# One group for the head sums and v pairs, a fifth product buffer, and one gate tile moved ahead of the second token group

## The chip, the cores and the metric

The kernel runs on one core of a Trainium2 chip. The metric is device time in microseconds (us) of one launch, as a median over runs of the same program. TensorE (PE) multiplies, VectorE (DVE) does elementwise work, ScalarE (ACT) does activations and moves results out of PSUM, GpSimd (POOL) does small statistics and issues some DMAs, and the queue of SyncE (SP) issues most other DMAs. Each engine runs its own instructions in program order.

## The reference

A layernorm of x (2048 tokens, 512 features) feeds two branches, and both are added to x. All arrays are bfloat16.

```python
xn = _layernorm(x)
return x + _A_ref(xn, A_wqkv, A_wo) + _B_ref(xn, B_w_in, B_w_sp, B_b_sp, B_w_out)

# A: 32 heads of 16 features, each token attends to 8 tokens: its own and those 2, 4, ... 14 before it
logits = einsum('bhsd,bhswd->bhsw', q, kg) * Dh ** -0.5   # masked where the index is below 0
o = einsum('bhsw,bhswd->bhsd', softmax(logits), vg)       # then o @ wo

# B: a gated unit that mixes over all tokens, Fh = 688
z = _gelu(x @ w_in)
z1, z2 = z[..., :Fh], _layernorm(z[..., Fh:])
g = einsum('ts,bsf->btf', w_sp, z2) + b_sp
return (z1 * g) @ w_out
```

## The kernel before

All data stays on the chip between load and store. The 2048 tokens are 16 tiles of 128; two halves (`th` 0 and 1) of 1024 tokens are used for attention, and four token groups (`b` 0 to 3) of 512 tokens for the q and k projections.

The order is written out by hand in two lists of short names, `ten` (lines 455 to 461, mostly PE and ACT work) and `vec` (lines 444 to 454, mostly DVE and POOL work). The function `advance` walks both lists; `needs` (line 464) says which names must have been recorded before another, and `do` (line 577) maps a name to its helper. So the order in `ten` is the order of PE and of ACT, and the order in `vec` is that of DVE and POOL. The hardware waits come from the buffers that the instructions read and write.

The names that matter here:

- `zN` is the matrix product of token tile N for z2 (line 209, 8 matmuls of 344 columns into one PSUM pair), `hN` its gelu on ACT (line 220), and `qN` the sum of its squares on ACT (line 225). `yN` is the product of tile N for z1 with its gelu (lines 244 to 246).
- `kBC` (line 254, 8 matmuls) projects token group B: C = 0, 1 are the two parts of q and C = 2, 3 the two of k. The helper copies the PSUM pair on ACT (line 256). `k1x` reads the transposed tiles 4 to 7.
- `vN` (line 269) projects a pair of v features in 32 matmuls, each of which uses 32 columns of the PE array at one of four positions (`tile_position`). ACT copies the result (line 271).
- `mTW`, `jTW`, `fTW`, `dTW`, `pTW`: the product of q with two shifted copies of k for half T and window pair W on DVE (line 289), and the adding up of the four feature chunks, by DVE (lines 292, 293) or with its first step as a DMA that POOL issues (`d`, line 298).
- `STW` (line 305) sums that product over the features of each head, with four matmuls that also use 32 columns each, and ACT moves the result (line 307) into `a_sb`. `xT` (line 315 on) is the softmax of half T, after its four head sums.
- `tN` is the DMA transpose of normalized tile N into `xnT` (line 205), `WN` a DMA transpose of two tiles of w_sp into one of three buffers `wsp` (line 368 on), `MN` the mixing product of output tile N (line 374), and `gN` the gate on DVE (line 382). `zsN` and `znN` are the statistics and the normalization of z2, by four tiles. `aT.N` are the twelve steps of attention of half T on DVE, and `Q`, `F` the output products and the additions of x.

PSUM is shared out by hand. Three pairs of banks `mm` are taken in turn by every z, k, v, y and M, and two banks `aux` in turn by the transposes at the start and by the head sums. So a z, k or v has to wait until ACT has emptied the pair taken three allocations earlier.

SBUF is full, so products share memory with other things. `prod` lists four homes, and `home` (line 277) says which one a product takes: two buffers of their own (0 and 1), the first 8192 columns of the z1 tile (2), and a part of the weights that is no longer read (3). The z1 tile has 16 x 768 = 12288 columns: it holds x in its first 8192 (`xs`) and normalized tiles in the other 4096 (`xn`) until they are transposed, and z1 later. A product that takes a home anew waits for the head sum of the product that had it.

```python
home = {(0, 0): 0, (0, 1): 1, (0, 2): 2, (0, 3): 0, (1, 0): 1, (1, 1): 0, (1, 2): 1, (1, 3): 3}
```

Of the kernel before, what the change touches and what calls it, by code (L numbers as in the profile page):

```python
# [7 lines left out]
BF16 = mybir.dt.bfloat16  # L8
# [5 lines left out]
P = 128  # L14
S = 2048
D = 512
NT = S // P
C = D // P
# [6 lines left out]
HS = S // 2  # L25
# [6 lines left out]
FP = (MF + 1) * P  # L32
# [6 lines left out]
def kernel(  # L39
# [22 lines left out]
    sb = ctx.enter_context(tc.tile_pool(name="sb", bufs=1))  # L62
# [35 lines left out]
    prod = [sb.tile([P, 2 * C * HS], BF16, name=f"prod{n}")[:] for n in range(2)]  # L98
    z2_r = sb.tile([P, NT * FH], BF16, name="z2")
    z2 = z2_r[:].rearrange("p (i f) -> p i f", i=NT)  # L100
    ot = [z2_r[:, n * D:(n + 1) * D] for n in range(12)]
    z1_r = sb.tile([P, NT * FP], BF16, name="z1")
    z1u = z1_r[:].rearrange("p (i f) -> p i f", i=NT)
    prod.append(z1_r[:, 0:2 * C * HS])
    prod.append(wts[:, C * FH:C * (FH + 4 * D)])
    xs = z1_r[:, 0:NT * D].rearrange("p (i d) -> p i d", i=NT)
    xn = [z1_r[:, NT * D + n * D:NT * D + (n + 1) * D] for n in range(8)]
    vp = sb.tile([P, DH, 2, HALO + GS], BF16, name="vp")
    a_sb = sb.tile([P, 2, W, GS], BF16, name="a_sb")
    wsp_r = [sb.tile([P, NT * 2 * P], BF16, name=f"wsp{n}") for n in range(3)]  # L110
    wsp = [r[:].rearrange("p (k t) -> p k t", k=NT) for r in wsp_r]

    mm = [ps.tile([P, 2, D], F32, name=f"mm{n}") for n in range(3)]
    aux = [ps.tile([P, D], F32, name=f"aux{n}") for n in range(2)]
# [159 lines left out]
        G.dma_start(vp[H:P, :, :, 0:HALO], vp[0:P - H, :, :, GS:GS + HALO])  # L274
        G.dma_start(vp[0:H, :, 1, 0:HALO], vp[P - H:P, :, 0, GS:GS + HALO])

    home = {(0, 0): 0, (0, 1): 1, (0, 2): 2, (0, 3): 0, (1, 0): 1, (1, 1): 0, (1, 2): 1, (1, 3): 3}

    def prod_ops(th, w2):
        pr = prod[home[th, w2]].rearrange("p (w c s) -> p w c s", w=2, c=C)  # L280
# [124 lines left out]
    def load_res(th):  # L405
        (SP if th else A).dma_start(xr[th], x2[th * HS:(th + 1) * HS, :].rearrange("(i p) d -> p i d", p=P))

    xr = [wsp_r[n][:].rearrange("p (i d) -> p i d", i=8) for n in (2, 0)]

    def gated_full(i, po, start, stop, cols=slice(0, D)):  # L410
        th, t0 = i // 8, (i % 8) * P
# [33 lines left out]
    for i in range(5, NT):  # L445
# [7 lines left out]
        a1.0 a1.1 g11 a1.2 a1.3 g12 a1.4 g13 a1.5 g14 a1.6 a1.7 g15 X1 a1.8 a1.9 F0 a1.10 a1.11 F1 F2  # L453
    """.split()
    ten = """
        T0 T1 B GL z0 z1 h0 T3 h1 z2 h2 z3 h3 LZ k00 k01 q0 k02 q1 k03 q2 z4 q3 h4 k10 k12 k11 k13
        W0 q4 k20 z5 h5 q5 k21 z6 h6 q6 k22 z7 h7 q7 k23 z8 h8 q8 k30 z9 h9 q9 k31 z10 h10 q10 S00 v0
        k32 z11 h11 q11 k33 z12 h12 q12 z13 h13 q13 v1 S01 S02 v2 z14 h14 z15 h15 q14 v3
        q15 v4 v5 v6 v7 S03 S10 y0 y1 M0 EL H e0 M1 EG y2 y3 y4 EL1 i0 EG1 M2 y5 y6 y7 y8 y9 y10 S11 S12 S13 M3 y11 M4 y12
        M5 W4 W5 y13 y14 y15 O4 EL2 e1 M6 O0 O1 M7 W6 i1 M8 O2 M9 W7 M10 O3 M11 M12 X0 M13 M14 M15 Q0 Q2 Q3  # L460
    """.split()
# [2 lines left out]
    def needs(n):  # L464
        k, a = n[0], n[1:]
        i = int(a) if a.isdigit() else 0
        if k == "T":
            return [f"n{i}"]
        if k == "z" and a.isdigit():
            return [[f"T{i}"], ["T1", "n2"], ["z1"], ["T3"]][i] if i < 4 else [f"t{i}"]  # L470
        if n == "GL":
            return ["T1"]
        if k == "q":
            return [f"h{i}"]
        if k == "h":
            return [f"z{i}"]
        if k == "k":
            last = 4 * int(a[0]) + 3
            return [f"T{last}" if last < 4 else f"t{last}"]
        if k == "v":  # L480
            return ["t15", "LW"]
        if k == "S":
            return ["p" + a]
        if k == "m":
            b = 2 * int(a[0])
            r = ([f"k{x}3" for x in (b, b + 1)] + ["K"]) if b else ["k03", "k12"] + (["k13"] if a != "00" else [])
            prev = [p for p in prods[:prods.index(n)] if home[int(p[1]), int(p[2])] == home[int(a[0]), int(a[1])]]
            return r + (["S" + prev[-1][1:]] if prev else []) + (["v7", "z15"] if a == "13" else [])
        if k == "j":
            return ["k13"]  # L490
        if k in "fdp":
            return ["m" + a]
        if k == "K":
            return ["k13"]
        if n[:2] == "zs":
            return [f"q{int(n[2:]) + x}" for x in range(4)]
        if k == "x":
            return [f"S{a}{w}" for w in range(4)]
        if k in "euic":
            return ["xeui"["euic".index(k)] + a]  # L500
        if k == "a":
            r = ["c" + a[0], "H", "S12"] + (["S13"] if a not in ("0.0", "0.1") else [])
            return r + ([f"y{x}" for x in range(NT)] if a[2:] == "11" else [])
        if k == "H":
            return [f"v{x}" for x in range(8)] + ["d12"]
        if k == "M":
            return [f"zn{x}" for x in range(NT)] + [f"W{i // 2}", "B"] + ([f"g{i - 3}"] if i >= 3 else [])
        if k == "g":
            return [f"M{i}", f"y{i}"]
        if k == "W":  # L510
            return [f"M{2 * i - 5}"] if i >= 3 else ["t15"]
        if k == "y":
            return [f"t{NT - 1}", "LW", "S02"]
        if k == "B":
            return ["T1"]
        if k == "O":
            return [f"y{x}" for x in range(NT)] + ["S13"]
        if k == "Q":
            return [["a0.11", "g7", "O4"], ["g7"], ["a1.11", "g15", "F0"], ["F2"]][i]
        if k == "F":  # L520
            return [f"Q{[0, 0, 2][i]}", f"X{i // 2}"]
        if k == "X":
            return ["M11" if i == 0 else "M13"]
        return []
# [171 lines left out]
    def advance(n):  # L696

        own = next(x for x in lists if n in x)
        while n not in done:
            first = next(x for x in own if x not in done)  # L700
            for x in needs(first):
                if x not in done:
                    assert x not in own, (first, x)
                    advance(x)
            do(first)
# [36 lines left out]
```

## Time and profile before

| | us |
|---|---|
| median of 3 runs | 202.16 (202.12 to 202.41) |
| the profiled execution, whole | 202.3 |
| its span, first to last instruction | 200.6 |
| PE busy | 195.9 |
| DVE busy | 175.7 |
| ACT busy | 96.0 |
| POOL busy | 38.7 |

The granted TensorE clock was 0.997 on average over the span. All times in the profile count from the start of the span; 1.7 us of the profiled execution lie around it. In the views, "PE mm L254 x8" is eight matmuls of line 254 that write a tile named mm, and a bracket at the end of a row of the timeline is the idle time of that engine ahead of it, with what ended the idle time. The chain of waits follows the work that ended last back to the beginning.

### The profile page before, as it was taken

How to read it: one execution, taken by the hardware profiler on the slowest of the kernel's cores; microseconds unless marked ns; L12 is line 12 of the kernel's file. 1: busy time of each engine (PE TensorE's matmuls, PEld its weight loads, DVE VectorE, ACT ScalarE, POOL GpSimd, SP SyncE). 2: the span in 40 equal slices, each digit the busy share in tenths (PEclk: the TensorE clock that was granted, in tenths of full speed). 3: DMA queues.
4: the chain of work that ended last, by engine and by line, in shares of the span. 5: the costliest groups of instructions: out<-in, count | busy, mean ns of one | idle time of the engine just before them, and what ended most of it. 6: DMA issues, size and time to landing. Idle time of an engine off the chain costs nothing.

```text
span 200.6 us, 3841 instructions
## 1 busy us (share of the span) xinstructions
PE 195.9 (98%) x1587; PEld 118.2 (59%) x1587; DVE 175.7 (88%) x192; ACT 96.0 (48%) x149; POOL 38.7 (19%) x62
## 2 busy tenths in 40 slices
PE   7999999999999999999999999999999999999993
PEld 2645555555656666666566666666666654444652
DVE  4887879999899799999979999999999799897333
ACT  3869879998998647885533264311222110000000
POOL 4366681138660431600000000000000000000000
PEclk9999999999999999999999999999999999999998
DMA  6999459399653837999979099996949611712023
GB/s 183 288 250 197 102 117 303 106 184 206 132 110 29 184 65 146 186 101 89 248 168 192 9 259 281 156 259 128 266 82 272 135 43 39 252 65 105 5 103 105
DMA packets 64289, 30.84 MB, mean 154 GB/s; under 512 B 53440, under 2 KB 62512, under 8 KB 64144
## 3 DMA queue, kind: packets, MB, share of 16 engines
q1 hardware_dynamic: 59296, 19.23, 46.4%
q0 software_dynamic: 1904, 6.59, 16.5%
q10 hardware_dynamic: 3072, 4.78, 8.8%
q8 instruction: 12, 0.20, 0.4%
q14 instruction: 5, 0.04, 0.1%
HBM read 10.03 MB, written 2.10 MB: 60 GB/s over the span
## 4 chain that ended last, share of the span: by engine, by line
PE 88%; DMA 6%; DVE 3%; POOL 1%; issue 0%
PE mm L374 37%; PE mm L209 16%; PE mm L254 10%; PE mm L269 7%; PE mm L413 7%; PE mm L425 5%; DMA z<-in_A_x_dram 4%; DMA xnT<-z 2%; PE aux L413 2%; DVE stats L182 1%; PE mm L562 1%; PE mm L419 1%; PE aux L305 1%; DVE z L196 1%; POOL rstd L187 1%; PE aux L562 0%
## 5 line engine op out<-in xcount | busy, mean ns | idle before, releaser
L374 PE MATMUL mm<-z,wsp 128*128 128x344 bf16 x512 | 75.7, 309 | 0.0
L374 PEld LDWEIGHTS <-wsp 128*128 128x128 bf16 x512 | 50.0, 98 | 24.9 <-issue 0.4
L209 PE MATMUL mm<-wts,xnT 128*128 128x344 bf16 x256 | 40.5, 309 | 0.0
L377 ACT ACTIVATE qk<-mm,b_col 128x688 bf16<-128x688 f32 x16 | 13.3, 834 | 49.8 <-PE mm L374 49.8
L347 DVE TENSOR_TENSOR prod<-vp,a_sb 128x4096 bf16<-128x4096 bf16 x16 | 36.0, 2284 | 0.0
L209 PEld LDWEIGHTS <-xnT 128*128 128x128 bf16 x256 | 24.6, 98 | 14.0 <-issue 0.8
L254 PE MATMUL mm<-xnT,wts 128*128 128x512 bf16 x128 | 29.1, 379 | 0.3 <-DMA xnT<-z 0.2
L289 DVE TENSOR_TENSOR prod<-qk 128x4096 bf16<-128x4096 bf16 (+1 forms) x14 | 27.1, 1979 | 0.1
L351 DVE TENSOR_TENSOR prod<-prod,prod 128x8192 bf16<-128x8192 bf16 x6 | 26.5, 4420 | 0.1
L254 PEld LDWEIGHTS <-wts 128*128 128x128 bf16 x128 | 14.3, 114 | 13.1 <-issue 0.9
L256 ACT CAST qk<-mm 128x1024 bf16<-128x1024 f32 x16 | 16.2, 1011 | 4.8 <-PE mm L254 3.0
L413 PE MATMUL mm<-wts,qk 128*128 128x512 bf16 (+1 forms) x65 | 14.7, 371 | 0.0
L269 PE MATMUL mm<-xnT,wts 128*32 128x512 bf16 x256 | 14.6, 381 | 0.0
L246 ACT ACTIVATE z<-mm 128x688 bf16<-128x688 f32 x16 | 11.8, 745 | 4.5 <-PE mm L209 4.5
L182 DVE BATCH_NORM_STATS2 stats<-z 128x6 f32<-128x512 bf16 x16 | 10.9, 683 | 3.4 <-DMA z<-in_A_x_dram 3.4
L413 PEld LDWEIGHTS <-qk 128*128 128x128 bf16 x85 | 8.1, 98 | 9.2 <-issue 0.6
L220 ACT ACTIVATE z<-mm 128x688 bf16<-128x688 f32 x16 | 11.9, 744 | 1.8 <-PE mm L209 1.8
L225 ACT ACTIVATE z_junk<-z 128x688 bf16<-128x688 bf16 x16 | 12.4, 778 | 0.3
L269 PEld LDWEIGHTS <-wts 128*32 128x32 bf16 x256 | 9.3, 139 | 4.6 <-issue 0.6
L430 DVE TENSOR_TENSOR z<-mm,wsp 128x512 bf16<-128x512 f32 (+1 forms) x8 | 5.0, 653 | 8.0 <-PE mm L425 4.8
L298 POOL DMA_DIRECT2D prod<-prod x8 | 7.1, 933 | 20.9 <-DVE prod L289 19.5
L425 PE MATMUL mm<-wts,xnT 32*128 32x512 bf16 x160 | 10.7, 375 | 0.0
(93 smaller groups left out, 186.2 us busy)
## 6 DMA issues: line engine op xcount, KB each, us to landing
prod<-prod POOLq DMA_DIRECT2D x8, 512.0 KB, 5.7
wts<-in_A_wo_dram ACTq DMA_DIRECT2D x4, 512.0 KB, 5.5
out_dram<-z SPq DMA_DIRECT2D x9, 128.0 KB, 1.7
z<-in_A_x_dram SPq DMA_DIRECT2D x4, 256.0 KB, 4.4
wts<-in_A_wqkv_dram SPq DMA_DIRECT2D x2, 512.0 KB, 7.0
z<-z POOLq DMA_DIRECT2D x2, 512.0 KB, 5.6
wsp<-in_A_x_dram ACTq DMA_DIRECT2D x1, 1024.0 KB, 6.3
wsp<-in_A_x_dram SPq DMA_DIRECT2D x1, 1024.0 KB, 5.3
```

The costliest lines, as they stand in the source:

```text
L182: V.bn_stats(stats[:, i, :], xs[:, i, :])
L209: PE.matmul(pz[:, hh, 0:FHALF], xnT[:, kc, i * P:(i + 1) * P], w_z2[:, hh, kc] if part else w_z1[:, kc, hh * FHALF:(hh + 1) * FHALF], star ...
L254: PE.matmul(pq[:, cc, :], w_c[:, kc], xnT[:, kc, t0:t0 + D], start=(kc == 0), stop=(kc == C - 1))
L256: A.copy(qk[b // 2][:, a, 2 * c2:2 * c2 + 2, o:o + D], pq[:])
L269: PE.matmul(pv[32 * g:32 * g + 32, dd, :], w, r, start=(kc == 0), stop=(kc == C - 1), tile_position=(0, 32 * g))
L289: ops.append(lambda ww=ww, k=k, c=c: V.tensor_tensor(pr[:, ww, c], q[:, c], k[:, c], ALU.mult))
L347: return lambda: V.tensor_tensor(dst, vp[:, :, th, off:off + GS], a_sb[:, th, w].unsqueeze(1).broadcast_to([P, DH, GS]), ALU.mult)
L351: return lambda: V.tensor_tensor(dst, dst, x, ALU.add)
L374: PE.matmul(pg[:, hh, 0:FHALF], w[:, k, (j % 2) * P:(j % 2 + 1) * P], z2[:, k, hh * FHALF:(hh + 1) * FHALF], start=(k == 0), stop=(k == NT ...
L377: A.activation(g.rearrange("p (a b) -> p a b", a=2), pg[:, :, 0:FHALF], ACT.Identity, bias=b_col[:, j:j + 1])
L413: PE.matmul(po[:, cols], uT[th][:, m, t0:t0 + P], wout[:, m, cols], start=(start and m == 0), stop=(stop and m == MF - 1))
L425: PE.matmul(pos[g], op[32 * g:32 * g + 32, th, d, s * P:(s + 1) * P], wo_r[32 * g:32 * g + 32, d, :], start=(start and d == 0), stop=(stop ...
```

## The change

Two things are reordered and the buffers are shared out anew.

In `ten`, z5 with its gelu moves ahead of the second token group's chunks (k10, k12, k11, k13), where z4 stood alone. Every later z keeps its distance to the k chunks and so comes one place earlier. The first half's head sums S00, S01, S02 and the v pairs v0 to v3, which stood in three places among the z and k of the last tiles, now all follow z15, just ahead of v4 to v7, S03 and S10. The squares q13, q14 and q15 are spread between the v pairs.

Product (0, 3) gets a new home 4. It takes the last 8192 columns of a z1 tile that is lengthened by 4096 columns: those of `xn` and those of the third w_sp buffer, which is now a part of this tile. The homes of (1, 0), (1, 1) and (1, 2) become 0, 1, 0 in place of 1, 0, 1. In `needs`, the load W2, which fills that third buffer first, now needs S03.

```diff
-    z1_r = sb.tile([P, NT * FP], BF16, name="z1")
-    z1u = z1_r[:].rearrange("p (i f) -> p i f", i=NT)
+    z1_all = sb.tile([P, NT * FP + NT * 2 * P], BF16, name="z1")
+    z1_r = z1_all[:, 0:NT * FP]
+    z1u = z1_r.rearrange("p (i f) -> p i f", i=NT)
     prod.append(z1_r[:, 0:2 * C * HS])
     prod.append(wts[:, C * FH:C * (FH + 4 * D)])
+    prod.append(z1_all[:, NT * D:NT * D + 2 * C * HS])
...
-    wsp_r = [sb.tile([P, NT * 2 * P], BF16, name=f"wsp{n}") for n in range(3)]
-    wsp = [r[:].rearrange("p (k t) -> p k t", k=NT) for r in wsp_r]
+    wsp_r = [sb.tile([P, NT * 2 * P], BF16, name=f"wsp{n}")[:] for n in range(2)]
+    wsp_r.append(z1_all[:, NT * FP:NT * (FP + 2 * P)])
+    wsp = [r.rearrange("p (k t) -> p k t", k=NT) for r in wsp_r]
...
-    home = {(0, 0): 0, (0, 1): 1, (0, 2): 2, (0, 3): 0, (1, 0): 1, (1, 1): 0, (1, 2): 1, (1, 3): 3}
+    home = {(0, 0): 0, (0, 1): 1, (0, 2): 2, (0, 3): 4, (1, 0): 0, (1, 1): 1, (1, 2): 0, (1, 3): 3}
...
-    xr = [wsp_r[n][:].rearrange("p (i d) -> p i d", i=8) for n in (2, 0)]
+    xr = [wsp_r[n].rearrange("p (i d) -> p i d", i=8) for n in (2, 0)]
...
     ten = """
-        T0 T1 B GL z0 z1 h0 T3 h1 z2 h2 z3 h3 LZ k00 k01 q0 k02 q1 k03 q2 z4 q3 h4 k10 k12 k11 k13
-        W0 q4 k20 z5 h5 q5 k21 z6 h6 q6 k22 z7 h7 q7 k23 z8 h8 q8 k30 z9 h9 q9 k31 z10 h10 q10 S00 v0
-        k32 z11 h11 q11 k33 z12 h12 q12 z13 h13 q13 v1 S01 S02 v2 z14 h14 z15 h15 q14 v3
+        T0 T1 B GL z0 z1 h0 T3 h1 z2 h2 z3 h3 LZ k00 k01 q0 k02 q1 k03 q2 z4 h4 z5 q3 h5 k10 k12 k11 k13
+        W0 q4 k20 z6 h6 q5 k21 z7 h7 q6 k22 z8 h8 q7 k23 z9 h9 q8 k30 z10 h10 q9 k31 z11 h11 q10
+        k32 z12 h12 q11 k33 z13 h13 z14 h14 q12 z15 h15 S00 v0 S01 S02 v1 q13 v2 q14 v3
         q15 v4 v5 v6 v7 S03 S10 y0 y1 M0 EL H e0 M1 EG y2 y3 y4 EL1 i0 EG1 M2 y5 y6 y7 y8 y9 y10 S11 S12 S13 M3 y11 M4 y12
...
-            return [f"M{2 * i - 5}"] if i >= 3 else ["t15"]
+            return [f"M{2 * i - 5}"] if i >= 3 else ["t15", "t15", "S03"][i:i + 1]
```

## The prediction

> **What bounds the kernel now.** I read the busy times first, then one window over the middle, then the chain of waits in order of time, and last the timeline of each engine where the change touches it.
>
> ```profile
> PE 195.9 (98%) x1587; PEld 118.2 (59%) x1587; DVE 175.7 (88%) x192; ACT 96.0 (48%) x149; POOL 38.7 (19%) x62
> ```
>
> ```profile
> 20.20:197.40 177.20, 177.19 (x1486) 108.46 (x1486) 160.77 (x147) 81.76 (x123) 28.60 (x30) 1.00 0.70 146
> ```
>
> The second fence is the window from 20.20 to 197.40 us: of 177.20 us PE is busy 177.19, at a granted clock of 1.00. No engine makes PE wait there. What can shorten this stretch is less PE time for the same matmuls, and ahead of it the little that PE loses before 20.20. The chain of waits (start, length, what) shows where that is:
>
> ```profile
> 15.06 5.00 DMA xnT<-z
> 20.07 0.14 issue
> 20.20 8.80 PE mm L254 x40
> ...
> 44.63 0.33 PE aux L305 x4
> 44.97 1.73 PE mm L269 x32
> 46.69 1.85 PE mm L254 x8
> 48.54 1.17 PE mm L209 x8
> 49.71 1.73 PE mm L254 x8
> 51.43 2.33 PE mm L209 x16
> 53.77 1.88 PE mm L269 x32
> 55.65 0.43 PE aux L305 x8
> 56.08 1.73 PE mm L269 x32
> 57.81 2.44 PE mm L209 x16
> 60.25 8.79 PE mm L269 x160
> 69.04 0.43 PE aux L305 x8
> 69.47 2.44 PE mm L209 x16
> ```
>
> Equal work has two lengths. Eight chunk matmuls (L254) take 1.73 us, but 1.85 right behind a v pair. A v pair (L269 x32) takes 1.73 behind another 32-column matmul, but 1.88 behind a z. Two z take 2.33, but 2.44 behind a v pair; five v pairs take 8.79 where 5 x 1.73 = 8.65. So each change between full-array and 32-column matmuls costs 0.11 to 0.15 us, while L269 to L305 and back costs nothing (0.43 for two head sums, then 1.73).
>
> **Removed: two visits to the 32-column form.** Before, PE goes there three times: S00 v0; v1 S01 S02 v2; v3 to v7 S03 S10. Afterwards it goes once, and the first entry (into S00) and the last exit (into y0) stay. Gone are the exits into k32 (1.85 - 1.73 = 0.12) and z14 (2.44 - 2.33 = 0.11), and the entries into v1 (1.88 - 1.73 = 0.15) and v3 (8.79 - 8.65 = 0.14): **0.52 us**. The bounds are four times the smallest and the largest of these, 0.44 and 0.60.
>
> The Trainium skill, "TensorEngine Tiling (Array Packing)", section "Tiling Modes", says that changing the tiling mode drains TensorE, and changing the tile alone does not. The rows agree in both respects; the page gives no duration.
>
> **Moved: z5 ahead of k10.**
>
> ```profile
> 20.20 1.03 PE L254 MATMUL mm<-xnT,wts 128*128 128x512 bf16 x4 [0.17 <-DMA xnT<-z]
> 12.40 2.51 SPq L205 DMA_TRANSPOSE xnT<-z x2
> DMA to landing us min/median/max: 3.2/4.7/6.2
> ```
>
> The first row is k10: PE stood for 0.17 us until tile 7 had landed (issued at 15.06, landed at 20.07 in the chain). The other two rows are the DMA transposes of tiles 5 and 6. The first is issued at 12.40 and lands by 12.40 + 6.2 = 18.6 at the latest, so z5 can start at z4's end, 20.03, and k10 at 21.20, when tile 7 is there. **0.17 us** are gone, between 0 and 0.17. The lateness goes nowhere else: k20 and k30, which need tiles 8 to 15, start 1.0 us later than before.
>
> **What hides the rest.** PE's matmuls are the same in number and shape. Four things must not become a new wait.
>
> *ACT in the first place.* Its order changes from q2 q3 h4 k10 k12 to q2 h4 q3 h5 k10 k12, one gelu more ahead of the k copies.
>
> ```profile
> 19.81 0.78 ACT L225 ACTIVATE z_junk<-z 128x688 bf16<-128x688 bf16 x1
> ...
> 44.67 0.74 ACT L220 ACTIVATE z<-mm 128x688 bf16<-128x688 f32 x1 [0.15 <-PE mm L209]
> ...
> 45.54 0.78 ACT L225 ACTIVATE z_junk<-z 128x688 bf16<-128x688 bf16 x1
> ...
> 46.32 0.58 ACT L307 ACTIVATE a_sb<-aux 128x512 bf16<-128x512 f32 x1
> 46.79 1.00 ACT L271 CAST vp<-mm 128x1024 bf16<-128x1024 f32 x1
> ```
>
> ```profile
> 25.76 2.35 DVE L289 TENSOR_TENSOR prod<-qk 128x2048 bf16<-128x2048 bf16 x2
> 29.03 1.27 DVE L241 TENSOR_SCALAR z<-z,zmean,zrstd 128x688 bf16<-128x688 bf16 x3 [0.92 <-POOL zrstd L235]
> ```
>
> From start to start a gelu takes 0.87 and a square 0.78 (44.67, 45.54, 46.32). From q2 at 19.81 that puts h4 at 20.59, q3 at 21.46, h5 at 22.24 and the copy of k10 at 23.0, just when k10 ends (21.20 + 1.73 = 22.93). k12 ends at 24.66 and its copy of 1.0 us at 25.7. DVE's first product m00 needs that copy and started at 25.76: it is just not later. If it were, the 0.92 us that DVE then waits for POOL take it up.
>
> *ACT in the merged group.* The new order there is h13 h14 q12 h15 S00 v0 S01 S02 v1 q13 v2 q14 v3 q15 v4. PE ended k33 at 51.43. Afterwards one z more lies ahead of it (1.17), but not S00, v0 and the exit (0.33 + 1.73 + 0.12), and 0.17 is saved, so it ends at 51.43 - 2.18 + 1.17 - 0.17 = 50.25, z15 at 53.75, S00 at 54.08, v0 at 55.81, and S02 starts at 56.02. ACT keeps up with z13 and z14 and starts h15 at about 54.3, S00's move at 55.1 and v0's copy at 55.9. S02 takes the aux bank that S00 leaves, free at 55.1 + 0.58 = 55.7: 0.3 us in hand. v3 needs v0's pair free at 56.9 and starts at 59.7. Behind v1, v2 and v3 ACT needs 1.01 + 0.78 per pair against 1.73 on PE, so about 0.06 a pair is lost, and over v4 to v7 regained: the margin stays at 2 us or more. I cost it at nothing; uncovered it costs what ACT is late beyond these margins.
>
> *DVE and the homes.*
>
> ```profile
> 24.92 2.53 SPq L205 DMA_TRANSPOSE xnT<-z x2
> ```
>
> ```profile
> 45.95 4.49 DVE L289 TENSOR_TENSOR prod<-qk 128x4096 bf16<-128x4096 bf16 x2
> 51.37 1.67 DVE L241 TENSOR_SCALAR z<-z,zmean,zrstd 128x688 bf16<-128x688 bf16 x4 [0.93 <-POOL zrstd L235]
> ...
> 54.08 1.21 DVE L293 TENSOR_TENSOR z<-z 128x2048 bf16<-128x2048 bf16 x1
> ...
> 55.99 4.49 DVE L289 TENSOR_TENSOR prod<-qk 128x4096 bf16<-128x4096 bf16 x2
> ...
> 65.77 1.22 DVE L293 TENSOR_TENSOR prod<-prod 128x2048 bf16<-128x2048 bf16 x1
> ```
>
> These are m03, the norms of tiles 4 to 7, p02, m10 and p10. With the old home 0, m03 would wait for S00, now at 54.08, which is 8.1 us late; home 4 takes that away. Its memory is free: the last two transposes that read xn are issued by 27.45 (first row), 18.5 us ahead of m03, and the third w_sp buffer is empty until W2. m10, now in home 0, needs S00 at 54.08 and starts at 55.99. S02 needs p02, done at 55.29, and is asked for at 56.02. S10 needs p10, done at 66.99, and is asked for at about 68.4. POOL's order is unchanged; its fold d03 only writes elsewhere.
>
> *SP, and all that follows.*
>
> ```profile
> 91.34 9.39 SPq L367 DMA_TRANSPOSE wsp<-in_B_w_sp_dram x2
> DMA to landing us min/median/max: 6.4/6.8/7.2
> ```
>
> ```profile
> 103.11 4.67 PE mm L374 x32
> ```
>
> ```profile
> 160.02 0.52 DVE L382 TENSOR_TENSOR z<-qk,z 128x688 bf16<-128x688 bf16 x1 [1.26 <-ACT qk L377]
> ```
>
> W2 is issued at 91.34, behind a DVE step that ends there and not behind S03 at 69, so its new wait costs nothing and nothing queued on SP behind it moves. M4 is the first to use it, at 103.11; the two loads issued here land within 7.2 us, so W2 is there by 98.5, and 0.7 us less leaves 3.9. Late in the kernel DVE itself waits 1.26 us for PE and ACT at gate 14, so a PE that is 0.7 us earlier finds DVE ready.
>
> **Sum.** 0.52 + 0.17 = 0.69 us, with bounds 0.44 and 0.77. Against the profiled execution that is a span of 200.6 - 0.7 = 199.9 and a whole of 202.3 - 0.7 = 201.6. That execution lies 0.14 above the median of 202.16, so against the median: **201.47 us**.
>
> **Rivals.** *The cost of a change of form stays* (202.0). The extra 0.11 to 0.15 might belong to new operands or banks and not to the form; then only 0.17 goes: 202.16 - 0.17 = 201.99. Against it: the v pair behind S02 changes both and takes 1.73.
>
> *ACT empties too slowly* (201.8). Eight v pairs and four head sums now come in one run, where before z or k broke it up. If ACT is 0.6 us later than worked out at S00, S02 waits 0.3 for its bank and the gain falls to 0.39. Beyond 2 us the v pairs would wait too. ACT's 0.15 of idle time in each period of z and k (44.67) speaks against a backlog.
>
> The Trainium skill, same page, section "PSUM Bottleneck", warns that tiling speeds up TensorE and not the emptying of PSUM. That is this rival; before, the five v pairs in a row at 60.25 took 8.65 beside the entry, so the trace does not bear it out at that length.
>
> *The later k copy sets DVE back* (203.2, slower). m00 has no margin of its own. From 29.03 to p02 DVE has one wait, 0.93 at 51.37 on POOL's statistics, which are late with it. A copy of k12 that ends after 26.7 (29.03 - 2.35) uses up the 0.92; 0.73 later, at 27.4, p02 passes 56.02 and PE waits at S02, with all v pairs behind it. To end slower than before by over 0.2% the copy must end after about 28.5, 2.8 us later than worked out. Were ACT two chunks late (2 x 1.73 = 3.46, so 29.2), PE would lose 29.2 - 27.4 = 1.8, less 0.69: 203.2. For it: ACT runs closely there. Against it: it needs two whole chunks.
>
> **How the numbers follow.** Forecast 0.67, form cost stays 0.12, ACT slow 0.11, k copy late 0.10. A measurement of this kernel tells about 0.2%, 0.4 us, from no change, so faster means below 201.76. The forecast is inside that; half of "ACT slow" is too. Faster 0.73, same 0.17, slower 0.10. The bounds of the sum give 201.39 to 201.72, and the runs before spread by 0.29 us, so the forecast's own range is 201.2 to 201.9; with the two small rivals it is 201.1 to 202.1, and the last case is left out.
>
> **What would show it.** In the chain of waits afterwards: v1 to v7 at 1.73 a pair with no 1.85 or 1.88 among the chunks and z (else the first rival); k10 right behind z5, with no wait for xnT; PE busy without a gap from about 18.7; S10 ending at about 68.8 in place of 69.47 and M0 starting at about 71.2. A wait of PE for ACT or for the move of aux at S02 shows the second rival. A start of m00 after 26.7, and PE waiting for DVE at S02, show the third. If PE is early at M0 and late again at M4 or at the output, a load or DVE has taken the gain back, and the forecast is wrong.

## The result, and the profile after

| | before | changed kernel |
|---|---|---|
| median, us | 202.14 (201.90 to 202.62, 6 runs) | 201.40 (201.11 to 201.57, 6 runs) |
| profiled execution, whole, us | 202.3 | 201.44 |
| its span, us | 200.6 | 199.7 |

The ratio is 0.9961, with a 95% interval of 0.9949 to 0.9973. The prediction said 201.47. The line numbers of the changed kernel are 4 higher: z is L213, k L258, v L273, S L309 and M L378.

The chain of waits of the changed kernel (start, length, what) answers to the one that was shown of before:

```profile
18.87 2.33 PE mm L213 x16
21.20 8.63 PE mm L258 x40
29.84 1.17 PE mm L213 x8
31.00 1.73 PE mm L258 x8
...
48.37 1.73 PE mm L258 x8
50.09 3.50 PE mm L213 x24
53.59 0.33 PE aux L309 x4
53.92 1.73 PE mm L273 x32
55.65 0.43 PE aux L309 x8
56.08 12.09 PE mm L273 x224
68.17 0.43 PE aux L309 x8
68.60 2.44 PE mm L213 x16
71.04 7.00 PE mm L378 x48
```

The 1.85 and the 1.88 are gone. Seven v pairs take 12.09, which is 7 x 1.73 but for 0.02, and the only extra lengths left are the entry at 53.59 (0.33 against half of 0.43) and the exit at 68.60 (2.44 against 2.33). k10 follows z5 at once, so 40 chunk matmuls take 8.63 where the row before had 8.80. S10 ends at 68.60, predicted about 68.8, and M0 starts at 71.04, predicted 71.2.

A window of the changed kernel (stretch, length, busy time by engine, granted clock, DMA) shows that PE has no gap, and the timeline of DVE and PE shows the three places at which I had looked for a new wait:

```profile
18.70:196.50 177.80, 177.80 (x1495) 109.60 (x1493) 160.75 (x147) 82.31 (x126) 29.10 (x31) 1.00 0.71 147
```

```profile
25.74 2.36 DVE L293 TENSOR_TENSOR prod<-qk 128x2048 bf16<-128x2048 bf16 x2 [1.39 <-ACT qk L260]
...
53.18 1.21 DVE L297 TENSOR_TENSOR z<-z 128x2048 bf16<-128x2048 bf16 x1
...
159.14 0.52 DVE L386 TENSOR_TENSOR z<-qk,z 128x688 bf16<-128x688 bf16 x1 [1.27 <-ACT qk L381]
```

```profile
55.47 0.39 PE L309 MATMUL aux<-prod,rsel 128*32 128x512 bf16 x4
55.69 0.39 PE L309 MATMUL aux<-z,rsel 128*32 128x512 bf16 x4
```

The first product m00 starts at 25.74, as worked out, but it now waits 1.39 us for the copy of k12: DVE was ready earlier in this execution. p02 ends at 54.39, and S02, which needs it, starts at 55.69, so 1.30 us are in hand. Late in the kernel DVE still waits 1.27 us at gate 14 (1.26 before): everything behind y0 has moved as a whole.

### The profile page after: what moved, and what is told of

Its sections match the earlier page's. It is cut to its first block, busy times and chain, and to the rows that moved or that the text cites. A ratio compares the mean times of both kernels' runs of the same rounds, so it can differ in the third digit from the quotient of the medians.

```text
span 199.7 us, 3843 instructions
## 1 busy us (share of the span) xinstructions
PE 195.2 (98%) x1587; PEld 119.0 (60%) x1587; DVE 175.7 (88%) x192; ACT 95.0 (48%) x149; POOL 39.0 (20%) x62
## 4 chain that ended last, share of the span: by engine, by line
PE 95%; DVE 1%; DMA 1%; ACT 0%; issue 0%
PE mm L378 37%; PE mm L213 19%; PE mm L258 14%; PE mm L273 7%; PE mm L417 7%; PE mm L429 5%; PE aux L417 2%; PE mm L566 1%; DMA z<-in_A_x_dram 1%; PE mm L423 1%; PE aux L309 1%; DVE stats L186 1%; PE aux L205 0%; PE aux L566 0%; ACT xnT L206 0%; DVE z L434 0%
## 5 line engine op out<-in xcount | busy, mean ns | idle before, releaser
L378 PE MATMUL mm<-z,wsp 128*128 128x344 bf16 x384 | 56.8, 309 | 0.0
L378 PEld LDWEIGHTS <-wsp 128*128 128x128 bf16 x384 | 37.5, 98 | 18.8 <-issue 0.4
L213 PE MATMUL mm<-wts,xnT 128*128 128x344 bf16 x256 | 40.3, 309 | 0.2 <-ACT xnT L206 0.2
L213 PEld LDWEIGHTS <-xnT 128*128 128x128 bf16 x256 | 24.7, 98 | 13.9 <-ACT xnT L206 0.5
L258 PE MATMUL mm<-xnT,wts 128*128 128x512 bf16 x128 | 29.1, 379 | 0.0
L293 DVE TENSOR_TENSOR prod<-qk 128x4096 bf16<-128x4096 bf16 (+1 forms) x12 | 22.7, 1930 | 1.4 <-ACT qk L260 1.4
L258 PEld LDWEIGHTS <-wts 128*128 128x128 bf16 x128 | 14.6, 114 | 11.9
L378 PE MATMUL mm<-z,z 128*128 128x344 bf16 x128 | 19.2, 309 | 0.0
L260 ACT CAST qk<-mm 128x1024 bf16<-128x1024 f32 x16 | 16.2, 1012 | 4.8 <-PE mm L258 3.8
L378 PEld LDWEIGHTS <-z 128*128 128x128 bf16 x128 | 12.5, 98 | 6.1
L273 PE MATMUL mm<-xnT,wts 128*32 128x512 bf16 x256 | 14.2, 379 | 0.0
L273 PEld LDWEIGHTS <-wts 128*32 128x32 bf16 x256 | 9.5, 138 | 4.3
L434 DVE TENSOR_TENSOR z<-mm,wsp 128x512 bf16<-128x512 f32 (+1 forms) x7 | 4.3, 649 | 8.0 <-PE mm L429 4.8
```

Source lines behind the costliest of these rows:

```text
L213: PE.matmul(pz[:, hh, 0:FHALF], xnT[:, kc, i * P:(i + 1) * P], w_z2[:, hh, kc] if part else w_z1[:, kc, hh * FHALF:(hh + 1) * FHALF], star ...
L258: PE.matmul(pq[:, cc, :], w_c[:, kc], xnT[:, kc, t0:t0 + D], start=(kc == 0), stop=(kc == C - 1))
L260: A.copy(qk[b // 2][:, a, 2 * c2:2 * c2 + 2, o:o + D], pq[:])
L273: PE.matmul(pv[32 * g:32 * g + 32, dd, :], w, r, start=(kc == 0), stop=(kc == C - 1), tile_position=(0, 32 * g))
L293: ops.append(lambda ww=ww, k=k, c=c: V.tensor_tensor(pr[:, ww, c], q[:, c], k[:, c], ALU.mult))
L378: PE.matmul(pg[:, hh, 0:FHALF], w[:, k, (j % 2) * P:(j % 2 + 1) * P], z2[:, k, hh * FHALF:(hh + 1) * FHALF], start=(k == 0), stop=(k == NT ...
```

## The experiments

Each kernel is compared with runs of the kernel before on the same chip. The kernel before had medians of 201.98 us beside the first four rows, 202.03 beside the next three and 202.09 beside the last four, so medians of different batches differ by a tenth or so for the same kernel. The ratio is the one on record; it is close to the ratio of the two medians but not the same.

| run | median, us | ratio to before | 95% interval |
|---|---|---|---|
| z5 alone | 202.01 | 1.001 | 0.9999 to 1.0022 |
| group alone | 201.58 | 0.998 | 0.9968 to 0.9991 |
| group split in three by two y | 202.06 | 1.0002 | 0.9991 to 1.0013 |
| homes alone | 201.92 | 1.0003 | 0.9993 to 1.0013 |
| new order, old homes | 209.99 | 1.0397 | 1.0378 to 1.0416 |
| one more z ahead of k10 | 201.49 | 0.9973 | 0.9962 to 0.9985 |
| two more z ahead of k10 | 202.49 | 1.0017 | 1.0001 to 1.0033 |
| before, again | 202.02 | 0.9997 | 0.9979 to 1.0016 |
| changed kernel, again | 201.55 | 0.9975 | 0.9956 to 0.9995 |
| late tile 7, k10 behind z4 | 201.34 | 0.9965 | 0.9944 to 0.9986 |
| late tile 7, k10 behind z5 | 201.42 | 0.9968 | 0.9951 to 0.9985 |

Since z4 starts at between 18.64 and 19.26 us in the profiles of these runs, I also compare PE's time from the start of z4 to the start of y0 in the chain of waits, which is free of that spread. It is 68.60 - 18.87 = 49.73 us in the changed kernel.

### The two parts, one at a time

The first run has only z5 and the later z moved, in the kernel before:

```diff
-        ... q2 z4 q3 h4 k10 k12 k11 k13 W0 q4 k20 z5 h5 ... k31 z10 h10 q10 S00 v0 k32 z11 ...
+        ... q2 z4 h4 z5 q3 h5 k10 k12 k11 k13 W0 q4 k20 z6 h6 ... k31 S00 v0 z11 h11 q10 k32 z12 ...
```

> The kernel before with z5 (and every later z one place earlier) ahead of the second token group's chunks; three visits to the 32-column form are kept. Theory A (the move is worth the distance between the start of z4 plus one z and the start of k10, that is 19.87 to 20.20 on PE's timeline, 0.33 us, because the wait also let the pipeline run empty): 0.33 us below the kernel before, about 201.8. Theory B (only the 0.17 us that the profile calls idle): 0.17 below, about 202.0.

It gained nothing: the interval excludes the 0.33 us, and 0.17 as well. Its chain of waits:

```profile
18.90 2.33 PE mm L209 x16
...
69.16 2.44 PE mm L209 x16
```

From z4 to y0 that is 50.26 us. The second run is the changed kernel with the z back in their old places, so that the group and the homes are left:

```diff
-        ... q2 z4 h4 z5 q3 h5 k10 k12 k11 k13 W0 q4 k20 z6 h6 q5 k21 ...
+        ... q2 z4 q3 h4 k10 k12 k11 k13 W0 q4 k20 z5 h5 q5 k21 ...
```

> The changed kernel without the move of z5: one group for v and S, new homes, but k10 right behind z4. Theory A (cost of the form: two entries and two exits at 0.11 to 0.15 us): 0.52 to 0.55 us below the kernel before, about 201.6, with k10 still waiting for tile 7. Rival (the gain is all from z5's move or from the homes): no different from before, 202.1.

It gained 0.40 us, with an interval of 0.18 to 0.65, which holds the 0.52 to 0.55 of theory A. Its chain of waits:

```profile
19.07 1.17 PE mm L213 x8
20.24 8.63 PE mm L258 x40
...
56.28 12.09 PE mm L273 x224
68.37 0.43 PE aux L309 x8
68.80 2.44 PE mm L213 x16
```

From z4 to y0 it takes 68.80 - 19.07 = 49.73 us, to the hundredth what the changed kernel takes, though its k10 stands right behind z4. The expected wait for tile 7 is not there: 19.07 + 1.17 = 20.24, and k10 starts at 20.24.

### Is tile 7 late in every execution?

> The kernel before once more, for another profile of its front. Theory (the wait of k10 for tile 7 belongs to single executions: the two kernels of the first experiments that keep k10 behind z4 did not show it): time as before, and z4 to y0 on PE takes about 50.3 us, without the wait, in place of 50.7. Rival (it is always there in this kernel): k10 again 1.5 us behind the start of z4 in place of 1.17.

The chain of the kernel before, in another execution:

```profile
18.91 1.17 PE mm L209 x8
20.08 8.63 PE mm L254 x40
...
53.48 1.88 PE mm L269 x32
...
57.52 2.44 PE mm L209 x16
59.96 8.79 PE mm L269 x160
68.75 0.43 PE aux L305 x8
69.18 2.44 PE mm L209 x16
```

There is no wait, and the 40 matmuls take 8.63 in place of 8.80. From z4 to y0 it takes 69.18 - 18.91 = 50.27 us. So the group alone is worth 50.27 - 49.73 = 0.54 us, and in the execution on which I predicted, the wait came on top of it. The other profiles agree: those with the old groups and no wait of PE take 50.26 or 50.27 (z5 alone, homes alone, before again), and those with the merged group and no wait take 49.72 or 49.73 (changed kernel, group alone, one more z, both with a late tile 7).

To force the wait I put the transposes of tiles 7 to 9 behind the statistics of tiles 9 and 10, in the grouped kernel without and with z5's move:

```diff
-    ... s8 r8 n7 t7 s9 r9 n8 t8 s10 r10 n9 t9 ...
+    ... s8 r8 s9 r9 s10 r10 n7 t7 n8 t8 n9 t9 ...
```

> The grouped kernel with k10 right behind z4, and with the normalization and transpose of tiles 7, 8, 9 put behind the statistics of tiles 9 and 10 on DVE: tile 7 is issued some 2.2 us later, at about 17.4, and lands at about 21. Theory (a late tile 7 stops PE at k10): PE waits 0.5 to 1.2 us for xnT, and the time is 202.1 to 202.8. Rival (landing does not follow the issue): 201.6.

> The changed kernel with the same late tile 7. Theory (z5 covers up to 1.17 us of lateness): no wait or little of it, 201.4 to 201.7, at least 0.5 us below the same kernel without the move of z5. Rival (the move is worth nothing even then): the same time as that one.

This failed as a test. Both ran in 201.34 and 201.42 us, not to be told apart, and k10 did not wait in the first. The rows on the tile xnT in the kernel without z5's move, in a window that holds the transposes of tiles 7 and 8, say why:

```profile
L209 SPq DMA_TRANSPOSE xnT<-z x2: 1190/1205/1220, 16.1 to 17.4; - x2
DMA to landing us min/median/max: 2.4/2.4/2.4
```

Tile 7 was issued at 16.1, not at 17.4, and landed in 2.4 us, at 18.5: earlier than in the first profile of before, where it was issued at 15.06 and took 5.0. So the edit moved the issue by less than planned, and the rival held too: the landing does not follow the issue. In the kernel with z5's move tile 7 was issued at 16.2 and took 3.4, so there was nothing to cover either.

In the changed kernel's own profile tile 7 was issued at 15.2 and took 5.0. It landed at 20.2, where a k10 right behind z4 would have started at 18.71 + 1.17 = 19.88, so z5 did cover a late tile there. The same holds in the profiles of the runs "group split in three" (20.4 against 20.13) and "new order, old homes" (19.8 against 19.65). With the first profile of before, that is four of the thirteen profiles in which tile 7 came too late for a k10 behind z4, by 0.1 to 0.3 us. What z5 is worth when tile 7 is late by more was not tried.

### Does the cost belong to the form?

```diff
-        ... q15 v4 v5 v6 v7 S03 S10 y0 y1 M0 ...
+        ... q15 v4 v5 y0 v6 y1 v7 S03 S10 M0 ...
```

> The changed kernel with y0 and y1 set between v5 and v6 and between v6 and v7: same matmuls, two more exits from and two more entries into the 32-column form, next to other operands and banks than before. Theory (each change of form costs 0.11 to 0.15 us whatever the neighbours): 0.52 us above the changed kernel, about 201.9, with rows of 1.88 for the v pairs behind a y. Rival (the cost belonged to the old operands or banks): same as the changed kernel, 201.4, and 1.73 for every v pair.

Chain of waits of this run:

```profile
56.33 8.63 PE mm L273 x160
64.96 1.27 PE mm L213 x8
66.24 1.88 PE mm L273 x24
68.12 1.27 PE mm L213 x8
69.40 1.89 PE mm L273 x32
71.28 0.43 PE aux L309 x8
```

Behind a v pair a y takes 1.27 where it takes 1.17 elsewhere, and behind a y a v pair takes 1.88 or 1.89 where it takes 1.73. (A few records of the middle pair are missing.) The neighbours are new, z1 weights and other banks; the cost is nearly the same: twice 0.10 for the exits and 0.15 and 0.16 for the entries, 0.51 us. The time is 202.06, 0.48 above the group alone on the same chip and 0.51 to 0.66 above the changed kernel's two medians in other batches, near the 0.52 expected, and all of the gain is gone.

### The homes

The homes and the longer z1 tile with the old order in `ten`:

> The changed kernel's buffers, homes and needs with the old order in the list ten. Theory (the homes only make room, they move no work): within 0.15 us of the kernel before, 202.1. Rival (the longer z1 tile or the waits on home 4 cost or win time): more than 0.3 us to either side.

The ratio is 1.0003, with an interval of 0.3 us at most to either side: no cost and no gain can be told. The other way round, the new order with the old homes:

```diff
-    home = {(0, 0): 0, (0, 1): 1, (0, 2): 2, (0, 3): 4, (1, 0): 0, (1, 1): 1, (1, 2): 0, (1, 3): 3}
+    home = {(0, 0): 0, (0, 1): 1, (0, 2): 2, (0, 3): 0, (1, 0): 1, (1, 1): 0, (1, 2): 1, (1, 3): 3}
```

> The changed kernel's order with the old homes: product (0, 3) in home 0 waits for S00, which now comes behind z15. Theory (the fifth home is what makes the group possible): the product starts at about 54.0 in place of 45.0, p02 ends at about 62.3, PE stands at S01 and S02 for about 6.4 us; 207.9, between 207 and 209. Rival (DVE has slack enough to hide it): 201.4.

The fifth home is what makes the group possible: without it PE stands at S01 and S02. But the time was 209.99, 2.1 us more than expected. PE's timeline, and windows (stretch, length, busy time of PE, weight loads, DVE, ACT, POOL, granted clock, DMA) of this run:

```profile
60.90 0.62 PE L309 MATMUL aux<-prod,rsel 128*32 128x512 bf16 x4 [5.48 <-DVE prod L297]
62.04 0.62 PE L309 MATMUL aux<-z,rsel 128*32 128x512 bf16 x4 [0.52 <-DVE z L297]
62.44 14.44 PE L273 MATMUL mm<-xnT,wts 128*32 128x512 bf16 x224
```

```profile
53.00:62.00 9.00, 3.04 (x43) 1.41 (x41) 8.26 (x9) 3.48 (x8) 1.76 (x2) 0.89 0.49 98
62.00:64.00 2.00, 1.96 (x20) 0.84 (x24) 1.86 (x4) 0.76 (x2) 1.38 (x1) 0.50 0.48 96
64.00:66.00 2.00, 2.00 (x24) 0.83 (x20) 2.00 (x2) 0.00 (x0) 1.92 (x2) 0.50 0.00 0
66.00:68.00 2.00, 2.00 (x36) 1.08 (x32) 1.06 (x2) 1.78 (x3) 1.86 (x1) 0.79 0.00 0
68.00:77.00 9.00, 9.00 (x176) 6.18 (x168) 7.68 (x15) 6.55 (x10) 2.11 (x2) 1.00 0.68 118
```

S02 ends 6.8 us later after z4 than in the changed kernel, near the 6.4 expected. The rest is the clock. PE stood from about 55.4; in finer windows the granted clock was 1.00 up to 60.0, 0.50 from there to 66.5, and 1.00 again from 67, and the seven v pairs take 14.23 us in the chain of waits in place of 12.09, 2.14 more. The Trainium skill, "TensorE: Matmul & The Clock Gate", Part 1, states that the clock gate halves PE's rate after an idle window of about 3.4 us and gives the full rate back after a busy window as long. This trace agrees in the 0.50, which began some 4.6 us into the wait; the full clock came back 4.5 to 5 us after S02 began, later than one such window.

### How near the third rival was

One more and two more z ahead of k10 push the copy of k12 back further:

```diff
-        ... z4 h4 z5 q3 h5 k10 k12 ...
+        ... z4 h4 z5 q3 h5 z6 h6 k10 k12 ...          (one more)
+        ... z4 h4 z5 q3 h5 z6 h6 z7 h7 k10 k12 ...    (two more)
```

> The changed kernel with z6 ahead of the second token group's chunks as well, all later z one place earlier again. The copy of k12 then ends at about 26.9 in place of 25.7 and m00 starts there. Theory (DVE's margin up to S02 is 1.3 us in the changed kernel's profile, from p02's end at 54.4 to S02 at 55.7): no loss, 201.4. Rival (no margin): 1.2 us longer.

> The changed kernel with z6 and z7 ahead of the second token group's chunks. The copy of k12 ends at about 28.05 and m00 starts 2.3 us later than in the changed kernel. Theory (margin 1.3 us, then one for one): PE waits 0.6 to 1.1 us at S02, 202.0 to 202.5. Rival (POOL's statistics or the later order on ACT give DVE the time back): 201.4.

Both came out as expected: 201.49 with one more, 202.49 with two. In the run with two, DVE's first product and PE's S02 read (timeline):

```profile
28.12 2.37 DVE L293 TENSOR_TENSOR prod<-qk 128x2048 bf16<-128x2048 bf16 x2 [3.99 <-ACT qk L260]
```

```profile
56.83 0.40 PE L309 MATMUL aux<-z,rsel 128*32 128x512 bf16 x4 [0.74 <-DVE z L297]
```

The times are those of the timelines, and "in hand" is what lies between the end of p02 and the start of S02:

| | m00 starts | p02 ends | S02 starts | in hand |
|---|---|---|---|---|
| group alone (k10 behind z4) | 24.77 | 53.43 | 55.89 | 2.46 |
| changed kernel | 25.74 | 54.39 | 55.69 | 1.30 |
| one more z | 26.87 | 55.52 | 55.66 | 0.14 |
| two more z | 28.12 | 56.77 | 56.83 | PE waits |

So z5's move takes 1.2 us of DVE's margin, and in the runs of z5 alone it gave nothing for it. That the margin matters was seen when the changed kernel was measured again:

> The changed kernel once more, beside the kernel before on the same chip. Theory (the gain is that of the form changes, with little or nothing from z5): 0.4 to 0.6 us below the kernel before. Prediction's sum: 0.69 below.

Its 12 runs had a median of 201.55, 0.54 below the kernel before. The interval of the ratio is a gain of 0.10 to 0.89 us, which holds both 0.54 and 0.69. The execution that was profiled there was the slowest of them, 202.62 us:

```profile
55.53 1.23 DVE L297 TENSOR_TENSOR z<-z 128x2048 bf16<-128x2048 bf16 x1 [1.53 <-DMA z<-z]
```

```profile
56.81 0.40 PE L309 MATMUL aux<-z,rsel 128*32 128x512 bf16 x4 [0.56 <-DVE z L297]
```

Its chain of waits ahead of that S02:

```profile
45.37 10.07 DMA z<-z
...
55.53 1.24 DVE z L297
```

The second of the two fold DMAs (`d02`) of product (0, 2), issued at 45.37, landed only at 55.44, so p02 was late and PE stood at S02 with all v pairs behind it: from z4 to y0 this execution took 69.73 - 19.26 = 50.47 us in place of 49.73. Why the DMA was slow is not shown. It is the place that the prediction named for its slower rival, reached by a DMA and not by ACT.

## Why the prediction was right, step by step

*What bounds the kernel* was right: PE, without a gap, at full clock. The gain of the group is PE time for the same matmuls. It reached the end undiminished: the two first profiles differ by 0.89 us from z4 to y0 and by 0.9 in their spans.

*The changes of form*, 0.52 us: right in kind and size. The measured difference from z4 to y0 is 0.54, the group alone gains 0.40 (0.18 to 0.65), and two extra round trips give it back. The first rival, that the cost belongs to operands or banks, fell with the split. What in the engine makes a change of form cost this, no run shows.

*z5 ahead of k10*, "0.17 us are gone, between 0 and 0.17": this term was mis-sized. In the execution that I read, the wait was 0.33 to 0.35, twice what I counted. From the start of z4 to that of k10 it is 20.20 - 18.70 = 1.50 us, 0.33 more than the 1.17 of a z. Before took 69.41 - 18.70 = 50.71 us on PE's timeline from z4 to y0, the changed kernel 68.53 - 18.71 = 49.82, a difference of 0.89, which less 0.54 for the group is 0.35. (0.17 of it showed as idle time. The row of z4's matmuls is 1.33 long and so covered the other half; the 8.80 in the prediction's own fence, where 40 chunk matmuls otherwise take 8.63, was a sign of it.) In the other executions with k10 behind z4, those of the runs "group alone", "homes alone", "before, again" and "late tile 7", it was zero, and z5 alone gained nothing in 12 runs. A wait that one execution shows is not a wait of every execution. For the median the lower end of the bound, 0, was the better value, though in single executions the move hides up to about 0.35.

*What hides the rest*: the ACT times came out within 0.1 us at the start (k12's copy at 24.70 to 25.71; the steps given for the copy of k10 add up to 23.11 and not to 23.0, and it started at 22.97). In the merged group S00's move ran 0.4 us earlier than worked out, at 54.67, and S02 had no wait for its bank: the second rival did not come. The homes cost nothing that can be told and were needed. W2, POOL and the output stage did not bite.

*The slower rival*: its place, S02 behind p02, was right, and its price too (two more z cost about 1 us). Its threshold was a little off. I put it at a copy of k12 that ends at 27.4; with one more z it ended at 26.84 and 0.14 us were left, so it lies at about 27.0.

*The number*: 201.47 against 201.40. That the two lie so close is partly luck. Of the 0.69 us, the 0.52 is shown; the 0.17 stood for a wait that was twice as long in the execution that I read and absent in the four other profiles that have k10 behind z4. The two comparisons of the changed kernel put its median 0.74 and 0.54 us below before, with intervals of 0.55 to 1.03 and 0.10 to 0.89; the form accounts for 0.54. Whether the 0.2 between them is z5 in some executions or the spread between runs is not settled. The run "late tile 7, k10 behind z4" speaks for the spread: beside the same runs of before as the second comparison it came out 0.75 below, without z5's move (its DVE order at the start differs as well).

## What to carry to other kernels

When an engine is full, look for the same instruction group at two lengths: the difference, by what stood ahead of it, is a cost of the order, and it can be had without less work. Before a small wait is counted as a gain, look for it in a second execution, above all where it depends on a DMA at the start. And count what a move takes from another engine's margin: here one step that gained nothing in the repeated runs took half of it.

## What the runs showed of the hardware that was not expected

- Behind a PE wait of 5.48 us (new order, old homes) seven v pairs took 14.23 us in place of 12.09, 2.14 more, since the granted clock stayed at 0.50 until past 66.5, more than 5 us after the wait had ended at 60.90.
- The DMA transpose of tile 7 landed after 5.0 us when it was issued at 15.06 (before), and after 2.4 us when it was issued at 16.1 (late tile 7, k10 behind z4). An accumulating DMA of 512 KB in SBUF (z<-z) took 5.6 us in the median on the page of before; in the profile of "changed kernel, again" the median of four was 9.1, and one took 10.07.
- A gap that the profile shows as 0.17 us of idle time was 0.33 us from start to start (20.20 - 18.70 - 1.17, before).
